# Conformer block on one core: eight input loads are moved behind other DMA reads on one queue

## The chip, the cores and the metric

The kernel runs on one core of a Trainium2 chip. Its engines work side by side, each through its own list of instructions: TensorE (PE, matrix products; PEld is its loading of weights), VectorE (DVE), ScalarE (ACT), GpSimd (POOL), and SyncE (SP), which here does nothing but issue DMA transfers. They wait for each other through semaphores. The metric is device microseconds of the whole program.

## The reference

One conformer block over x of shape (2, 4000, 144): two batches of 4000 tokens of 144 features, 4 heads of 36.

```
x = x + 0.5 * (silu(layernorm(x) @ w_ff1a) @ w_ff1b)
q, k, v = split(layernorm(x) @ w_qkv)               # 4 heads of 36
x = x + softmax(q k^T * 36**-0.5) v @ w_o           # 4000 x 4000 scores per head
a, b = split(layernorm(x) @ w_pw1)
c = depthwise_conv(a * sigmoid(b), dw)              # 5 taps along the tokens
x = x + silu(c) @ w_pw2
x = x + 0.5 * (silu(layernorm(x) @ w_ff2a) @ w_ff2b)
return layernorm(x)
```

## The kernel before

**Tiles.** Tokens are cut into 16 chunks of 500, chunks 0 to 7 for the first batch and 8 to 15 for the second; a chunk is four blocks of 125 tokens on 125 partitions. All of x lies on the chip in one tile X. Each chunk goes through layer norm, the first feed-forward and the q, k, v products ("pre"), then attention, then convolution and the second feed-forward. Attention is by far the largest part: TensorE makes scores (PS<-QT,KT), ScalarE, and for a part of the tiles VectorE, makes exponentials out of them (PT<-PS), and TensorE multiplies those with the values (PS<-PT,VA). While the attention of the first chunks runs, the pre of later chunks is worked in between, and while the first batch's attention runs, the second batch's pre.

**Transposes.** TensorE needs the normalized chunk (XN, or AN for the attention's output) with features on partitions. After the first chunks this is done through DRAM by `blocks` (line 967): VectorE transposes 32 x 32 squares in place (STREAM_TRANSPOSE XN<-XN); SP then issues four DMA writes into a DRAM buffer `rows` (the order in which it stands there does the rest of the transposing), waits for them to land, and issues the DMA reads that bring the chunk back, two for each chunk. For the feed-forward and the convolution the reads go to a tile XT, one of five; for the q, k, v products to XTQ, one place for each of the eight chunks of a batch. All of these, the X loads and the output go out on SP's one queue, in SP's order.

**X loads.** Chunks 0 to 7 are loaded at the very start. Those of the second batch stand in the list `later` (line 837), in the order 9, 10, 8, 11, 12, 14, 15, 13. `blocks` counts its calls in `n_dma`. From the fourth call on, each call issues one load of the list, behind its four writes and ahead of its two reads:

```
for a in range(4): ...            # four writes  rows <- XN
n_dma[0] += 1
if n_dma[0] > 3 and later:
    load_x("sp", later.pop(0), cost=0.0, lat=0.0)
yield need("sp")
for dst, f0, f1, n, cost, lat in reads: ...   # two reads  XT or XTQ <- rows
```

The reads wait for the writes' semaphore; an X load waits for nothing but its turn on SP.

**Order.** Work is described by generators (threads) that a planner interleaves by modelled costs when the program is built. The order on each engine is then permuted by a table, ORDER (`R.reorder`, line 2039), so that on the chip each engine has a fixed list; nothing is decided at run time. An X load belongs to the same step as the writes or reads that it is emitted with, and is permuted with them. The recorder emits every instruction from one line, so the profile shows L377 for nearly all; tiles and operations tell them apart.

Of the kernel before, what the change touches and what calls it, by code (L numbers as in the profile page):

```python
# [133 lines left out]
def c_dve(n, rate=1.0):  # L134
    return n / (960 * rate) + 0.07
# [398 lines left out]
def bass_standalone__conformer_family_zipformer__speech_kernel(  # L534
# [258 lines left out]
    def load_x(eng, c, r=(), cost=0.45, lat=2.9):  # L793
        op(eng, "dma_start", X[0:TB, c * NB:(c + 1) * NB, :], x_tok[c], q=f"x{c}", r=r, w=[("X", c, i) for i in range(NB)],
           cost=cost, lat=lat)

    def load_ff(eng, qa, qb, WA, WE, WB, wa, wb, nm, la=None, lb=None):
        load_k(eng, qa, WA, wa[:, 0:512], (nm, "a", 0), (nm, "z", 0), la)
        load_k(eng, qa, WE[:, :, 64:128], wa[:, 512:FF], (nm, "a", 1), (nm, "z", 1), la)
        load(eng, qb, WB[:, 0:4, :], wb[0:512, :].rearrange("(t p) d -> p t d", p=128), [(nm, "b", 0)], lat=lb)  # L800
        load(eng, qb, WB[0:64, 4, :], wb[512:FF, :], [(nm, "b", 1)], lat=lb)
        load(eng, qb, WB[64:128, 5, :], wb[512:FF, :], [(nm, "b", 2)], lat=lb)
# [31 lines left out]
        load("sp", "w2", WP2Z[i * LC:(i + 1) * LC, i, :], w_pw2[ML:D, :], [("WP2Z", i)])  # L834
    load("sp", "w2", DWR[0:KCONV, 0:D], dw, ["DWR"])
    load_ff("sp", "w2", "w2", WA2, WE2, WB2, w_ff2a, w_ff2b, "W2")
    later = [9, 10, 8, 11, 12, 14, 15, 13]
    n_dma = [0]
    R.free["sp"] += 0.45 * len(later)

# [126 lines left out]
    def blocks(v, key, z, reads, q, wk):  # L967
        yield need("dve")
        op("dve", "transpose", v, v, r=[key], w=[key], cost=c_dve(320))
        yield need("sp")  # L970
        first, v = None, v.rearrange("p (g k n) -> p g k n", g=2, n=32)
        for a in range(4):
            args = "sp", "dma_start", DR[z, :, :, a, :, :].rearrange("k r g n -> r g k n"), v[32 * a:32 * a + 32, :, :, :]
            if first is None:
                first = op(*args, q=f"d{z}", r=[key], w=[("DR", z)], cost=W_COST, lat=W_LAT)
            else:
                R.more(first, [key], [("DR", z)], *args, q=f"d{z}", cost=W_COST, lat=W_LAT)
        n_dma[0] += 1
        if n_dma[0] > 3 and later:
            load_x("sp", later.pop(0), cost=0.0, lat=0.0)  # L980
        first, d = None, DR[z, :, :, :, :, :].rearrange("k r a g n -> (k r) g a n")
        yield need("sp")
        for dst, f0, f1, n, cost, lat in reads:
            args = "sp", "dma_start", dst, d[f0:f1, :, :, :].rearrange("f g a n -> f g (a n)")[:, :, 0:n]
            if first is None:
                first = op(*args, q=q, r=[("DR", z)], w=wk, cost=cost, lat=lat)
            else:
                R.more(first, [("DR", z)], wk, *args, q=q, cost=cost, lat=lat)

    def transp_q(u, c, bs, inter):  # L990
        cc, n = c % CPB, len(bs)
        wk = [("XTQ", cc, i) for i in bs]
        q_inter[c] = inter
        if inter:
            yield from blocks(
                XNF[:, u, :], ("XN", u), NXT + cc,
                [(XTQF[0:HD, k, cc, :, :], HD * k, HD * k + HD, TB, 0.855, 2.2) for k in range(2)], f"tq{cc}", wk)
            return
        bk = yield need("pe", banks, dur=0.11 * n)
        ps = PSH[0:HD, bk, 0:256 * n].rearrange("p (k i n) -> p k i n", k=2, i=n)  # L1000
        for k in range(2):
            for i in range(n):
                op("pe", "transpose", ps[:, k, i, 0:TB], XN[0:TB, u, i, k * HD:(k + 1) * HD], IDENT[0:TB, 0:TB],
                   r=[("XN", u), "ID"], w=[("ps", bk)], cost=0.055, kind="f")
        yield need("dve", hold=True)
        c0 = cc * CH + bs[0] * TB
        copy(XTQ[0:HD, :, c0:c0 + n * TB].rearrange("p k (i n) -> p k i n", i=n), ps[:, :, :, 0:TB], [("ps", bk)], wk,
             2 * n * TB, 2.0, flex())
        banks.give(bk)

    def transp(u, an, s, bs, inter, dma, rows=TB):
        n, key = len(bs), ("AN" if an else "XN", u)
        wk = [("XT", s, i) for i in bs]
        x_inter[s] = dma
        if dma and s not in xt_set:
            xt_set.add(s)
            op("pool", "memset", XT[0:LP, s, 1, :, :], 0.0, w=wk, cost=0.5)
        if dma:
            yield from blocks((ANF if an else XNF)[:, u, :], key, s,
                              [(XTF[0:128, s, 0, :, :], 0, 128, 128, 0.43, T_LAT), (XTF[0:16, s, 1, :, :], 128, D, 128, 0.43, T_LAT)], f"t{s}", wk)  # L1020
            return
        bk = yield need("pe", banks, dur=0.11 * n)
        ps = PSH[:, bk, 0:256 * n].rearrange("p (k i n) -> p k i n", k=2, i=n)
        kr = (128, 32 if inter else LP)
        for k in range(2):
            for i in range(n):
                b = bs[i] if an else i
                if inter:
                    src = (ANI if an else XNI)[0:rows, u, b // 2, 128 * k:128 * k + kr[k], b % 2]
                else:  # L1030
                    src = (ANS if an else XNS)[0:rows, u, b * D + 128 * k:b * D + 128 * k + kr[k]]
                op("pe", "transpose", ps[0:kr[k], k, i, 0:rows], src, IDENT[0:rows, 0:rows], r=[key, "ID"],
                   w=[("ps", bk)], cost=0.055, kind="s" if inter and k else "f")
        eng = flex()
        for k in range(2):
            yield need(eng, hold=True)
            copy(XT[0:kr[k], s, k, bs[0]:bs[-1] + 1, 0:rows], ps[0:kr[k], k, :, 0:rows], [("ps", bk)], wk, n * rows, 2.0,
                 eng)
        banks.give(bk)
# [1031 lines left out]
```

## Time and profile before

| | us |
|---|---|
| runs of the kernel before | 888.76, 888.76, 889.62 (median 888.76) |
| profiled execution, its own time | 894.72 |
| its span, first to last instruction | 892.8 |

| engine | busy us | share of the span | instructions |
|---|---|---|---|
| PE | 862.4 | 97% | 11478 |
| ACT | 852.4 | 95% | 1095 |
| DVE | 818.5 | 92% | 1799 |
| POOL | 303.2 | 34% | 584 |

Mean granted TensorE clock: 0.990.

How to read it: "busy" of PE counts a product from its start to its modelled end, at whatever clock was granted. A timeline row has its start, its length, the engine, the operation as out<-in, how many were merged, and in brackets the idle time just before it and what ended that. In the chain of waits "SPq" is SP issuing, "DMA" is a transfer on its way. A row of the table by stretches has the stretch, its length, then the busy time of PE, PEld, DVE, ACT and POOL with their instructions, and at the end the granted TensorE clock (1.00 is full), the mean busy share of the 16 DMA engines, and GB/s.

### The profile page before, as it was taken

To read this page: it belongs to the slowest core of one execution; us is meant where nothing else is said; L and a number is where in the kernel's file an instruction comes from. 1 tells how busy PE (TensorE), PEld (TensorE's weight loads), DVE (VectorE), ACT (ScalarE), POOL (GpSimd) and SP (SyncE) were. 2 spreads that over 40 slices of the span, in tenths; PEclk is the share of its full clock that TensorE was granted. 3 is DMA by queue.
4 is the path that set the end of the run, shared out by engine and by line. 5 is a ranking of instruction groups with operands and counts; after the bars stand their busy time and mean duration, and the time that the engine had idled before them with its cause. 6 is when DMAs were issued, how large, how long until landed. Compare 5 with 4: busy or idle time off the path is not lost.

```text
span 892.8 us, 27130 instructions
## 1 busy us (share of the span) xinstructions
PE 862.4 (97%) x11478; PEld 385.8 (43%) x11478; DVE 818.5 (92%) x1799; ACT 852.4 (95%) x1095; POOL 303.2 (34%) x584
## 2 busy tenths in 40 slices
PE   8989999999999999999999999999999999999996
PEld 7533333344344444344344444443434343444466
DVE  7956999999999999999988899998888999999987
ACT  6778999999999999999999999999999999999974
POOL 7761510214433333114106224241541017021733
PEclk9988999999999999999999999999999999999999
DMA  3230110111210210201101111002111001101101
GB/s 101 47 79 21 43 36 18 22 22 31 51 30 22 44 30 18 55 16 38 36 16 25 34 29 31 22 16 43 30 37 23 8 10 42 36 9 36 36 17 34
DMA packets 114222, 28.81 MB, mean 32 GB/s; under 512 B 101085, under 2 KB 114100, under 8 KB 114100
## 3 DMA queue, kind: packets, MB, share of 16 engines
q1 hardware_dynamic: 112642, 26.46, 13.5%
q8 instruction: 90, 1.47, 0.7%
q10 hardware_dynamic: 1458, 0.62, 0.3%
q14 instruction: 32, 0.26, 0.1%
HBM read 13.44 MB, written 13.61 MB: 30 GB/s over the span
## 4 chain that ended last, share of the span: by engine, by line
ACT 44%; PE 38%; DVE 15%; POOL 1%; DMA 1%; issue 1%; SPq 1%; DVEq 0%
ACT PT L377 39%; PE PS L377 38%; DVE PT L377 8%; ACT TH L377 4%; DVE ST L377 1%; DVE X L377 1%; DVE QT L377 1%; DVE XN L377 1%; DVE HT L377 1%; POOL XN L377 1%; DVE KT L377 1%; POOL RS L377 1%; SPq L377 1%; DMA X<-in_x_dram 0%; DVE AN L377 0%
## 5 line engine op out<-in xcount | busy, mean ns | idle before, releaser
L377 ACT ACTIVATE PT<-PS 128x1000 bf16<-128x1000 f32 (+1 forms) x822 | 756.6, 1066 | 10.8 <-PE PS L377 9.6
L377 PE MATMUL PS<-QT,KT 64*64 64x500 bf16 x3968 | 427.4, 387 | 14.0 <-ACT PT L377 8.3
L377 PE MATMUL PS<-PT,VA 64*37 64x500 bf16 x4712 | 412.1, 374 | 2.0 <-DVE PT L377 0.7
L377 DVE TENSOR_SCALAR PT<-PS 128x500 int16<-128x500 f32 x372 | 244.3, 668 | 8.0 <-PE PS L377 6.5
L377 PEld LDWEIGHTS PS<-QT,KT 64*64 64x64 bf16 x3968 | 124.7, 104 | 241.5 <-ACT PT L377 135.0
L377 POOL TENSOR_SCALAR RS<-ST 125x4 f32<-125x4 f32 x130 | 35.2, 271 | 467.3 <-DVE ST L377 461.1
L377 PEld LDWEIGHTS PS<-PT,VA 64*37 64x37 bf16 x4712 | 141.1, 96 | 97.0 <-DVE PT L377 21.4
L377 POOL TENSOR_SCALAR XN<-X,RS 125x144 bf16<-125x144 bf16 x260 | 152.7, 621 | 7.4 <-DMA out_dram<-XN 0.7
L377 DVE TENSOR_SCALAR PT<-PT 128x1000 uint16<-128x1000 uint16 x372 | 150.6, 416 | 1.9 <-PE PS L377 0.5
L377 DVE TENSOR_TENSOR PT<-PT 128x1000 bf16<-128x1000 bf16 x186 | 126.3, 681 | 1.4
L377 ACT ACTIVATE TH<-PS 128x500 bf16<-128x500 f32 (+3 forms) x198 | 105.0, 553 | 4.5 <-PE PS L377 3.2
L377 POOL TENSOR_TENSOR RS<-RS,NHALF 125x4 f32<-125x4 f32 (+1 forms) x93 | 91.5, 987 | 37.4 <-DVE RS L377 31.5
L377 DVE SCALAR_TENSOR_TENSOR HT<-TH,PS 128x500 bf16<-128x500 bf16 (+1 forms) x135 | 80.7, 616 | 17.3 <-ACT TH L377 16.4
L377 PE MATMUL PS<-XT,WA 128*128 128x500 bf16 (+4 forms) x288 | 75.3, 366 | 0.4
L377 DVE BATCH_NORM_STATS2 ST<-X 125x6 f32<-125x288 bf16 x160 | 65.5, 445 | 2.9 <-DMA X<-in_x_dram 2.7
L377 DVE SCALAR_TENSOR_TENSOR X<-PS,X 125x288 bf16<-125x288 f32 (+1 forms) x128 | 57.1, 451 | 10.0 <-PE PS L377 8.9
L377 PE MATMUL PS<-WB,HT 128*125 128x144 bf16 (+1 forms) x640 | 51.9, 230 | 0.6 <-ACT HT L377 0.4
L377 PEld LDWEIGHTS PS<-WB,HT 128*125 128x125 bf16 (+1 forms) x640 | 44.2, 136 | 14.0 <-issue 4.8
L377 PEld LDWEIGHTS PS<-XT,WA 128*128 128x128 bf16 (+1 forms) x288 | 21.2, 98 | 34.4 <-issue 12.8
L377 POOL COPY U<-U 128x2 bf16<-128x2 bf16 (+1 forms) x54 | 11.6, 254 | 71.4 <-DVE U L377 71.4
L377 PE MATMUL PS<-U,DG 128*128 128x375 bf16 (+6 forms) x204 | 29.0, 264 | 0.2 <-DVE PT L377 0.2
L377 DVE STREAM_TRANSPOSE XN<-XN 128x320 f32<-128x320 f32 x54 | 27.0, 499 | 1.7 <-POOL XN L377 1.6
(93 smaller groups left out, 535.4 us busy)
## 6 DMA issues: line engine op xcount, KB each, us to landing
rows<-XN SPq DMA_DIRECT2D x216, 40.0 KB, 2.0
XT<-rows SPq DMA_DIRECT2D x56, 128.0 KB, 2.0
rows<-AN SPq DMA_DIRECT2D x60, 40.0 KB, 2.0
X<-in_x_dram SPq DMA_DIRECT2D x16, 140.6 KB
XTQ<-rows SPq DMA_DIRECT2D x26, 70.3 KB
out_dram<-XN SPq DMA_DIRECT2D x13, 140.6 KB
XT<-rows SPq DMA_DIRECT2D x56, 16.0 KB, 1.9
out_dram<-XN SPq DMA_DIRECT2D x3, 70.3 KB
```

The costliest lines, as they stand in the source:

```text
L377: ins = getattr(eng, o.name)(*o.a, **o.k)
```

## The change

The load no longer stands between a transpose's writes and its reads. It stands behind the reads, and each load of the list now carries the number of the call of `blocks` from which it may go: 9, 10 and 8 at the eighth call, 11 at the eleventh, 12 and 14 at the thirteenth, 15 at the fifteenth, 13 at the sixteenth.

```diff
-    later = [9, 10, 8, 11, 12, 14, 15, 13]
+    later = [(9, 8), (10, 8), (8, 8), (11, 11), (12, 13), (14, 13), (15, 15), (13, 16)]
...
     # blocks(), behind the four writes
-        n_dma[0] += 1
-        if n_dma[0] > 3 and later:
-            load_x("sp", later.pop(0), cost=0.0, lat=0.0)
     # the two reads
...
+        n_dma[0] += 1
+        while later and later[0][1] <= n_dma[0]:
+            load_x("sp", later.pop(0)[0], cost=0.0, lat=0.0)
```

In the order on SP, where the trace of before has a load behind the writes that start at 41.59, 48.96, 52.10, 59.63, 62.81, 90.25, 100.60 and 122.47 us, there is none now. Chunks 9, 10 and 8 follow one another behind the XTQ reads of 67.13, 11 stands behind the XT reads of 126.43, 12 and 14 behind those of 159.87, 15 behind the XTQ reads of 179.53 and 13 behind the XT reads of 199.20. The lists of PE, DVE, ACT and POOL hold the same operations in the same order; at a few places two of the XN buffers are exchanged.

## The prediction

> **What bounds the kernel now.** I read the page first, then busy time by stretches, then the chain of waits and the timelines of the queues around the one odd place. The page:
>
> ```profile
> span 892.8 us, 27130 instructions
> ...
> PEclk9988999999999999999999999999999999999999
> ...
> ACT 44%; PE 38%; DVE 15%; POOL 1%; DMA 1%; issue 1%; SPq 1%; DVEq 0%
> ```
>
> ScalarE and TensorE share the chain that ended last; DMA is 1% of it. TensorE's granted clock dips once inside the program (third and fourth slice of 22.3 us) before the end. Cut into stretches (columns: time of PE, PEld, DVE, ACT, POOL, then granted clock):
>
> ```profile
> 58.10:60.34 2.24, 0.00 (x1) 0.01 (x1) 0.46 (x1) 1.21 (x2) 2.24 (x3) 0.91 0.41 125
> 59.94:73.60 13.66, 13.26 (x130) 4.43 (x130) 4.84 (x9) 7.43 (x9) 1.50 (x2) 0.50 0.33 75
> 73.60:76.33 2.73, 2.73 (x30) 0.80 (x26) 1.18 (x3) 2.57 (x5) 0.00 (x0) 1.00 0.00 0
> 76.33:850.00 773.67, 757.06 (x10264) 318.44 (x10252) 728.37 (x1529) 769.51 (x945) 241.66 (x455) 1.00 0.13 29
> ```
>
> TensorE does nothing for 2.24 us, then runs 13.66 us at a clock of 0.50, busy throughout. From 76.33 to 850 ScalarE is busy 769.51 of 773.67 us: there the kernel is bound by ScalarE's work in its fixed order, and what that stretch begins with, it ends with. So a microsecond won before 76.33 is a microsecond at the end. What ScalarE lost before that:
>
> ```profile
> L377 ACT ACTIVATE PT<-PS 128x1000 bf16<-128x1000 f32 x8 | 7.8, 1003 | 6.2 <-PE PS L377 6.2
> L377 ACT ACTIVATE TH<-PS 128x500 bf16<-128x500 f32 x3 | 1.7, 588 | 0.5 <-PE PS L377 0.5
> L377 ACT ACTIVATE KT<-PS 128x500 bf16<-128x500 f32 x1 | 0.6, 587 | 0.3 <-PE PS L377 0.3
> ```
>
> These are ScalarE's groups between 61.9 and 76.3: 10.1 us of work with 7.0 us of idle time, all ended by TensorE.
>
> The first wait has its cause in the SP queue. The chain of waits there, then TensorE's own rows:
>
> ```profile
> 54.04 1.60 SPq L377
> ...
> 57.17 3.12 DMA XTQ<-rows
> ```
> ```profile
> 57.71 0.38 PE L377 MATMUL PS<-QT,KT 64*64 64x500 bf16 x4
> 60.34 1.02 PE L377 MATMUL PS<-XTQ,WK 72*128 72x500 bf16 x2 [2.24 <-DMA XTQ<-rows]
> ```
> ```profile
> 74.67 0.63 PE L377 MATMUL PS<-XT,WA 128*128 128x500 bf16 x2
> ```
>
> TensorE was ready at 58.10 (57.71 + 0.38) and waited for the XTQ read that landed at 60.29.
>
> **The change, part by part.** Eight X loads move on SP; no other engine's order changes. SP, in order of time:
>
> ```profile
> 48.96 2.55 SPq L377 DMA_DIRECT2D rows<-XN  x4
> 51.55 0.51 SPq L377 DMA_DIRECT2D X<-in_x_dram  x1
> 52.10 3.54 SPq L377 DMA_DIRECT2D rows<-XN  x4
> 55.69 0.51 SPq L377 DMA_DIRECT2D X<-in_x_dram  x1
> 56.23 3.35 SPq L377 DMA_DIRECT2D XTQ<-rows  x4
> ...
> 67.13 1.69 SPq L377 DMA_DIRECT2D XTQ<-rows  x2
> 90.25 2.60 SPq L377 DMA_DIRECT2D rows<-XN  x4
> ...
> 199.20 0.82 SPq L377 DMA_DIRECT2D XT<-rows  x2
> 206.91 2.55 SPq L377 DMA_DIRECT2D rows<-XN  x4
> ```
> ```profile
> 50.49 0.50 DVE L377 STREAM_TRANSPOSE XN<-XN 128x320 f32<-128x320 f32 x1
> ```
>
> *What it removes.* The X loads at 51.55 (chunk 10) and 55.69 (chunk 8) stand between the writes and the reads of the two transposes that TensorE waits for. Without the first, the second write may start at 51.55: its data was ready at 50.99. That is 0.55. Those four issues took 3.54 where an undisturbed write takes 2.55 (the row at 48.96); the chain shows the 1.60 of the last one. I put that on the load just ahead of it, so 0.99 goes. Without the second load another 0.54. The read is then issued at 56.23 - 0.55 - 0.99 - 0.54 = 54.15.
>
> How long it takes is bounded from both sides. Four such issues take 3.35, so the second of the pair goes out 0.84 later, at 54.99. The nearest rows for its landing are the same read in this trace, behind a load (3.12 after its issue, 57.17 to 60.29), and the undisturbed reads of the other transposes, the XT reads at 29 to 31 us:
>
> ```profile
> DMA to landing us min/median/max: 1.9/1.9/1.9
> ```
>
> So it lands between 56.9 and 58.1. I take 57.5, the middle: it is a read of other shape than XT's, but the load that delayed it is gone. TensorE needs it at 58.10, so at either end the 2.24 us go whole or to within 0.1.
>
> *The half clock.* It begins at 59.94, 1.84 us into TensorE's only long wait. I take the wait as its cause: without it, TensorE runs through this stretch at 1.00. The rule that speaks against this is in the Trainium skill, "TensorE: Matmul & The Clock Gate", section "Why this matters for your kernels": no gaps over about 3 us, since "One MID window of idle" drops the clock. Its Part 1 also has the full clock back after one busy window of about 3.4 us. By the rule a gap of 2.24 us would not do it, and a drop would cost some 1.7 us, an estimate from that page; at most 2.24 + 1.7 = 3.9 us would be won. The trace differs on both: 1.84 us idle came just before the drop, and 13.66 us followed. The measurement decides here.
>
> *The two together.* On TensorE, what was 58.10 to 76.33 (18.23 us) becomes half of 13.26 plus 2.73, that is 9.36, if nothing else limits it: 8.9 us less. ScalarE sets the nearer limit:
>
> ```profile
> 57.34 1.97 ACT L377 ACTIVATE PT<-PS 128x1000 bf16<-128x1000 f32 x2
> ...
> 85.48 44.93 ACT L377 ACTIVATE PT<-PS 128x1000 bf16<-128x1000 f32 x49
> ```
>
> It was done with its last exponential at 59.31 and reached 76.33 in 17.02 us. Undisturbed its eight PT take 44.93 / 49 = 0.917 each, 7.3 us; with 2.3 for TH and KT that is 9.6. So 17.02 - 9.6 = 7.4 us are won. The bound from above is TensorE's 8.9; from below, if only the wait goes and the clock stays, 2.24.
>
> *What is late next.* The read of the next transpose (XT, used by TensorE at 74.67) stands behind the SP write whose data comes from these two VectorE steps, which themselves waited for TensorE:
>
> ```profile
> 61.39 0.68 DVE L377 CAST KT<-PS 128x500 bf16<-128x500 f32 x1 [2.84 <-PE PS L377]
> 61.99 0.50 DVE L377 STREAM_TRANSPOSE XN<-XN 128x320 f32<-128x320 f32 x1
> ```
>
> In the changed kernel: cast at 58.10 + half of 1.05 = 58.6, transposed 0.60 + 0.50 later at 59.7, written by 62.3, second read issued 0.4 later (two took 0.82 at 199.20) and landed 1.9 after that, 64.6. TensorE comes there at 58.10 + 6.63 + 1.07 (74.67 less 73.60) = 65.8. Margin 1.2 us: I count nothing for it, but it is thin.
>
> *What it adds.* Three X issues (1.6 us on SP) right behind the XTQ read at 67.13. The next write behind them waits until 90.25, so SP stands idle for 21.4 us there, and both ends move alike. The other five go behind reads at later places; the tightest is the one behind 199.20, with 6.9 us until the next write. A load is quick against that, and needed late:
>
> ```profile
> 0.74 3.75 DMA X<-in_x_dram
> ```
> ```profile
> 97.46 0.81 DVE L377 BATCH_NORM_STATS2 ST<-X 125x6 f32<-125x288 bf16 x2
> ```
> ```profile
> 222.25 0.77 DVE L377 BATCH_NORM_STATS2 ST<-X 125x6 f32<-125x288 bf16 x2
> ```
>
> 97.46 is the first use of any of the three (chunk 8). Even with no lead they land by 68.82 + 1.6 + 3.75 = 74.2, 23 us before it, and both move alike. 222.25 is the first use of the fourth (chunk 11) and of any later one; the last of the eight is issued behind the read at 199.20. All this costs nothing; if the cover were gone, VectorE would wait in its fixed order and all behind it. The loads that stood after 76.33 stood where ScalarE hardly starves, by the stretch above, and the remaining ones before it delay reads that TensorE doesn't wait for here, so I count no gain for them.
>
> *Sum.* -2.24 and the half clock, together -7.4 at ScalarE; nothing added. Against the profiled execution's own 894.72 (span 892.8 and 1.9 around it) that is 887.3. The runs shown have a median of 888.76, 6.0 under the profiled one; I carry the difference over: 888.76 - 7.4 = 881.4.
>
> **The rivals.**
>
> *The clock is not won.* (a) The gap is not the cause of the half clock: 1.84 us are too short for it, something else halves the clock all the same, and ScalarE stays starved by it. Only the wait goes: 888.76 - 2.24 = 886.5. Against: one drop inside the program and one wait of this length in these rows, side by side. (This is what the skill's rule above would make of it.) (b) The runs shown never had the half clock: 6.0 us under the profiled run is close to what it costs. Then again only the wait goes, 886.5. For: that closeness. Against: the gap comes from the queue's order, which every run shares, and the three times lie within 0.9 us.
>
> *The read comes late anyhow.* If the 1.60 us issue and the 3.12 us read come from the transposes' own traffic, only the two load issues go (1.09): the read lands at 60.29 - 1.09 = 59.2, a wait of 1.1 us stays, and if the clock falls over it too, about 1 us is won: 887.7, hardly to be told from no change (a measurement of this kernel can tell about 0.2%, 1.8 us).
>
> *Slower.* The half clock moves to the XT read of 64.6 against 65.8. Should it land 3.0 us later than worked out, TensorE waits 1.8 us, as long as what came before the drop in this trace. If the runs shown had no half clock before, they get one: half of 13.26, less the wait that went: 888.76 + 6.6 - 2.24 = 893.1. For: the margin is 1.2 us and the chain runs through three engines. Against: no load is left near it, and its steps are short.
>
> **How the numbers follow.** The forecast, 881.4, has a chance of 0.62; (a) 0.08 and (b) 0.14, both at 886.5; the late read 0.08; slower 0.08. The likeliest case alone spans 878.1 (TensorE's 8.9 us, and for each of the two medians the 0.86 by which the runs shown differ) to 882.6 (the 1.2 us of the thin margin gone). The range reaches on to 886.5 and half that 0.86: 878.1 to 887.0, leaving out 0.16. Faster by over 0.2% is 0.62 + 0.22 = 0.84, within 0.2% 0.08, slower 0.08.
>
> **What would show it.** Right: SP's XTQ read issued near 54.2, no wait of TensorE over 0.5 us between 57 and 66, a granted clock of 1.00 from 50 to 80, ScalarE's idle time there near zero, and its long run of exponentials (85.48 here) some 7 us earlier. Wrong: a clock of 0.50 anywhere before the end, TensorE waiting on XT near 65, VectorE waiting on an X load, or the lead shrinking between 76 and 850.

## The result, and the profile after

The changed kernel takes 887.5 us (median of 14 runs, 887.03 to 888.41). The kernel before, run beside it 14 times, took 888.53 to 895.17, median 890.75; the ratio is 0.9958, with a 95% interval of 0.9942 to 0.9975. So it is faster, by much less than forecast, and 887.5 lies above the range. The two profiled executions differ by what was forecast: 894.72 before, 887.44 after, 7.28 us against 7.4. By their times, the three runs of before that the forecast started from (median 888.76) and this profiled execution belong to two different groups of runs, as the clocks of later runs show; most of what follows is about that.

Of the page of the changed kernel:

```profile
span 885.6 us, 27130 instructions
...
PEclk9999999999999999999999999999999999999999
...
ACT 43%; PE 39%; DVE 14%; POOL 1%; DMA 1%; SPq 1%; issue 1%; DVEq 0%; POOLq 0%
```

The dip of TensorE's clock in the third and fourth slice is gone. By stretches (the columns of before), before's 0.50 is now 1.00 and ScalarE is busy 13.46 us where it was 7.43:

```profile
59.94:73.60 13.66, 13.42 (x193) 5.18 (x192) 8.53 (x16) 13.46 (x17) 1.76 (x2) 1.00 0.32 76
```

ScalarE's groups between 61.9 and 76.3; the 7.0 us of idle time are 0.2:

```profile
L377 ACT ACTIVATE PT<-PS 128x1000 bf16<-128x1000 f32 x14 | 13.2, 1044 | 0.2 <-PE PS L377 0.2
L377 ACT ACTIVATE TH<-PS 128x500 bf16<-128x500 f32 x4 | 2.4, 646 | 0.0
L377 ACT ACTIVATE KT<-PS 128x500 bf16<-128x500 f32 x1 | 0.6, 593 | 0.0
```

SP's timeline after, then two pieces of its chain of waits, then TensorE's rows that waited for a DMA:

```profile
49.22 5.20 SPq L377 DMA_DIRECT2D rows<-XN  x8
54.46 4.15 SPq L377 DMA_DIRECT2D XTQ<-rows  x4
```
```profile
54.46 1.68 SPq L377
...
56.18 2.56 DMA XTQ<-rows
```
```profile
58.79 0.59 PE L377 MATMUL PS<-XTQ,WK 72*128 72x500 bf16 x2 [0.44 <-DMA XTQ<-rows]
69.96 0.59 PE L377 MATMUL PS<-XTQ,WK 72*128 72x500 bf16 x2 [0.24 <-DMA XTQ<-rows]
```

The eight writes stand without a load between them, the read goes out at 54.46, but its first issue takes 1.68 us, and 0.44 of the 2.24 us of waiting is left. ScalarE's long run of 69 exponentials, before and then after, starts 7.14 us earlier and is as long:

```profile
85.48 62.45 ACT L377 ACTIVATE PT<-PS 128x1000 bf16<-128x1000 f32 x69
```
```profile
78.34 62.43 ACT L377 ACTIVATE PT<-PS 128x1000 bf16<-128x1000 f32 x69
```

### The profile page after: what moved, and what is told of

Same layout as the page of the kernel before. It is cut to its first block, busy times and chain, and to the rows that moved or that the text cites. A ratio compares the mean times of both kernels' runs of the same rounds, so it can differ in the third digit from the quotient of the medians.

```text
span 885.6 us, 27130 instructions
## 1 busy us (share of the span) xinstructions
PE 857.2 (97%) x11478; PEld 385.1 (43%) x11478; DVE 818.4 (92%) x1799; ACT 851.5 (96%) x1095; POOL 303.9 (34%) x584
## 4 chain that ended last, share of the span: by engine, by line
ACT 43%; PE 39%; DVE 14%; POOL 1%; DMA 1%; SPq 1%; issue 1%; DVEq 0%; POOLq 0%
ACT PT L377 39%; PE PS L377 39%; DVE PT L377 8%; ACT TH L377 4%; DVE ST L377 1%; DVE HT L377 1%; DVE X L377 1%; POOL XN L377 1%; DVE QT L377 1%; DVE XN L377 1%; DVE KT L377 1%; SPq L377 1%; DMA XTQ<-rows 1%; POOL RS L377 0%; DVE VA L377 0%
```

## Experiments

My first theory: a wait of TensorE that is long enough halves its clock, whatever work is in it, and before has such a wait in some of its executions only. Its rivals: the half clock comes from something else in that stretch, or every execution of before has it. The expectations stand as they were given, ahead of each group of runs.

**Before again.** No edit.

> The kernel before, unchanged, run again. Theory A (a lottery over the clock): TensorE's wait of about 2.2 us at the XTQ read is there in every execution, but the half clock follows only in some, by where the wait falls in the clock's window. Then the runs form two groups, near 889 us with a mean granted clock of about 0.998 and near 893 to 895 us with about 0.990, and nothing between 890.5 and 891.5 that lacks a lower clock. Theory B (the spread is not the clock): the times between 888.5 and 895 do not follow the granted clock. If the profiled execution is one without half clock, theory A expects it to show the wait of about 2.2 us and a time near 889 us.

Measured: 889.9 median of 12 (888.44 to 894.46), ratio 0.9995 (0.9973 to 1.0018). It is two groups: seven runs at 888.44 to 889.97 with a mean granted clock of 0.998 or 0.999, five at 892.68 to 894.46 with 0.991 or 0.992. Over all 105 runs of before that stood beside the experiments, 59 had a clock of 0.996 or more and took 887.63 to 889.98, 41 took 892.5 to 895.0, and 5 lay between at 0.993 or 0.994. The profiled execution had the half clock. By stretches:

```profile
57.35:60.76 3.41, 1.19 (x18) 0.23 (x6) 1.00 (x2) 1.88 (x3) 3.41 (x5) 1.00 0.38 115
60.76:71.01 10.25, 10.25 (x112) 3.76 (x112) 4.05 (x7) 5.95 (x7) 0.60 (x2) 0.50 0.41 94
```

The first row is the 3.41 us just before the drop (TensorE busy 1.19, idle 2.22), the second the drop, 10.25 us long: three times 3.41. In the trace of before it was 13.66, four times.

**The wait filled, and made longer.** e3: before, with 32 products that nobody reads put into TensorE's list ahead of the product that waits. e9: 26 more ahead of the next wait, for XT. e8: before, with loads 11 and 12 also ahead of the first XTQ read.

```diff
+    fill_wait(R, "tq3", 32, IDENT)   # e3, e9: unread products ahead of the one that waits for XTQ
+    fill_wait(R, "t1", 26, IDENT)    # e9 alone: the same ahead of the one that waits for XT
```
```diff
-    # load behind the writes of each call from the fourth on: 9, 10, 8, 11, 12, 14, 15, 13
+    mid = {4: [9], 5: [10], 6: [8, 11, 12], 9: [14], 10: [15], 11: [13]}     # e8
```

> The kernel before with 32 products of 128 x 128 that nobody reads put ahead of the one that waits for the XTQ read, so TensorE is busy for about 1.8 of the 2.2 us. The read, and with it the loss to ScalarE, stays. Theory A: a granted clock of about 0.998 in every run, all runs between 888.3 and 890 us, none above 891; slower than the changed kernel's 887.5 by 1 to 2 us. Theory B: runs up to 895 us as before.

> The kernel before with unread products put ahead of both waits, 32 ahead of the first XTQ read and 26 ahead of the XT read behind it. Theory A: no window with over 1.3 us of idle time, so no half clock in any run: clock 0.997 or more throughout, one group at 888.3 to 889.8 us, where the kernel filled at the first wait alone had 888.6 to 891.6 and the kernel before 888.3 to 894.8. The late reads themselves stay, so it does not reach the changed kernel's 887.5.

> The kernel before with the loads of 11 and 12 moved to stand behind that of 8, ahead of the first XTQ read: two more issues and transfers there, none behind the next transposes. Theory A: the wait grows from 2.2 to 4 us or more, longer than one clock window of 3.41 us, so that some window has over 1.5 us of idle time wherever it begins: a granted clock of 0.990 to 0.993 in every run, no run near 889, all at 893 to 897 us. If the clock were no matter of the wait's length, the same two groups as before, each later by 2 us.

e3: 889.48 (888.6 to 891.62), ratio 0.9984 (0.9966 to 1.0003). No run above 891.62, but five at 890.9 or more, which I had not expected. Its profiled execution shows why: the filled wait was gone, and TensorE waited at the next late read, which halved the clock for one step of 3.41 us:

```profile
70.53 1.85 PE L377 MATMUL PS<-XT,WA 128*128 128x500 bf16 x4 [1.74 <-DMA XT<-rows]
```
```profile
66.88:70.29 3.41, 1.91 (x23) 0.61 (x22) 1.54 (x3) 2.76 (x4) 0.00 (x0) 1.00 0.39 116
70.29:73.71 3.42, 3.19 (x20) 1.08 (x24) 1.35 (x2) 1.89 (x3) 0.00 (x0) 0.50 0.05 14
```

e9, with both waits filled: 890.15 (889.46 to 891.26), ratio 0.9991 (0.9972 to 1.0011), one group with clocks of 0.997 to 0.999 in all 12 runs. Of the 105 runs of before, 46 had 0.994 or less. The loads stood where they were, and SP went on to issue the two reads late: in the profiled execution the first XTQ read at 55.68 and the first XT read at 66.96 (54.46 and 63.94 in the changed kernel, 56.23 and 66.17 in before). Only TensorE had no gap, with at most 0.04 us idle in any step of 3.41 between 53 and 74 us. That takes the loads' place in the queue and the DMA traffic out as direct causes of the half clock. It lies 1.8 us above the runs of before beside it that had no half clock (median 888.39), more than expected: the fillers take time of their own. e8: 895.38 (893.91 to 895.78), ratio 1.0045 (1.0026 to 1.0063), the half clock in all ten runs (0.990 to 0.992). The wait had been expected at 4 us or more and was 3.05:

```profile
61.60 0.60 PE L377 MATMUL PS<-XTQ,WK 72*128 72x500 bf16 x2 [3.05 <-DMA XTQ<-rows]
```

With a longer wait the half clock came in every run, with no gap in none: the wait is the cause.

**Parts of the change.** e1: only 9, 10 and 8 moved. e2: only the five others moved. e5 and e6: the changed kernel with one load put back behind its writes.

```diff
+    mid = {7: [11], 8: [12], 9: [14], 10: [15], 11: [13]}   # e1; later = [(9, 8), (10, 8), (8, 8)]
+    mid = {4: [9], 5: [10], 6: [8]}                         # e2; later without these
+    mid = {5: [10]}                                         # e5; later without 10
+    mid = {6: [8]}                                          # e6; later without 8
```

> Only the loads of chunks 9, 10 and 8 go behind the XTQ reads of the eighth call; 11, 12, 14, 15 and 13 stay between writes and reads as before. Theory A1 (the loads of 10 and 8 ahead of the first XTQ read are all of it): 887.5 us, clock 0.998, as the changed kernel. Theory A2 (TensorE, no longer held at the first XTQ read, meets the next late reads, XT and XTQ behind the loads of 11 and 12): a wait of 1.5 to 2.5 us there, at about 66 us, some runs at half clock, 888.5 to 894 us. Theory C (the later loads bring the gain): 889 to 894 us with the wait at the first XTQ read as before.

> The other half: 9, 10 and 8 stay between writes and reads as before, 11, 12, 14, 15 and 13 go behind reads as in the changed kernel. Theories A1 and A2: the wait of about 2.2 us at the first XTQ read stays, and with it the two groups, near 889 and near 893 to 895 us. Theory C: 887.5 us in every run.

> The changed kernel with one load, chunk 10, put back between the writes of the two transposes (where it stood at 51.55). The prediction's term for it is 0.55 for the issue and 0.99 for the slowed write, 1.5 us at the read: then TensorE waits 0.44 + 1.5 = 1.9 us at the first XTQ read, ScalarE is 1.5 us later, fast runs near 889.0 us, and some runs fall to half clock (893). Rival: the slowed write is made up by what SP and the read wait for anyway; then only 0.5 us at most, a wait under 1.0 us, 887.5 to 888.0 us, and no half clock.

> The changed kernel with one load, chunk 8, put back right ahead of the first XTQ read (where it stood at 55.69). The prediction's term: 0.54 for the issue and up to 1.2 for the read behind it. If the two terms add up, this one and that of chunk 10 together make the 1.7 us (2.14 less 0.44) by which the wait is longer with both, so here 0.44 + 0.2 to 0.7. If they do not add up, this load alone makes a wait of 1.5 us or more, 888.5 to 889 us, with half clock in some runs.

e1: 890.58 (888.43 to 893.6), ratio 0.999 (0.9971 to 1.0009). With the first wait gone, TensorE waits for XT behind loads 11 and 12, and six of 12 runs lie at 891.0 or more, with clocks of 0.992 to 0.997:

```profile
68.52 1.09 PE L377 MATMUL PS<-XT,WA 128*128 128x500 bf16 x4 [1.62 <-DMA XT<-rows]
```

So the loads between 59 and 66 us, for which I counted no gain, are needed: moving the front three alone gives no gain that these runs can tell. At the first XTQ read e1 did what the prediction said: SP's first issue took 0.89, the second read went out at 55.22 and landed at 57.60, and TensorE did not wait for it. e2: 888.22, ratio 0.9982 (0.9959 to 1.0005), eight runs at 887.62 to 888.85, four at 892.65 to 893.55. Its profiled execution had the whole wait and no half clock, because the wait fell across the border of two steps of 3.41 us, with 1.31 idle in the one and 0.83 in the other:

```profile
60.45 0.59 PE L377 MATMUL PS<-XTQ,WK 72*128 72x500 bf16 x2 [2.14 <-DMA XTQ<-rows]
```
```profile
56.20:59.62 3.42, 2.11 (x26) 0.77 (x24) 1.70 (x4) 3.32 (x5) 3.24 (x7) 1.00 0.37 92
59.62:63.03 3.41, 2.58 (x25) 0.71 (x27) 1.66 (x3) 1.60 (x2) 2.01 (x2) 1.00 0.38 83
```

(The borders are counted back in steps of 3.413 us from the clock's drop at the end. The step is worked out from the traces' clock records, whose stretches between two changes are whole multiples of it: 10.24 us is three, 13.65 four, 54.61 sixteen.) e5: 887.91, ratio 0.9974 (0.9955 to 0.9993), one run of 12 with the half clock, a wait of 0.79; e6: 887.38, ratio 0.9972 (0.9956 to 0.9989), a wait of 0.50 at this place, which the profile puts down to VectorE, and no run with the half clock. One load put back costs 0.4 us or nothing, where I had expected more of load 10. With both (e2) the wait was 2.14 us, but e2's profiled execution, like e5's, also has a slow write (1.56 and 1.39 us instead of 0.6), which the next runs show to come by chance.

**Why only some executions.** Before twice more, for a profiled execution without the half clock; e10 is one.

> The kernel before, unchanged, one profiled execution, to see one without the half clock. If the half clock falls on about half of all executions, this one has either no dip inside the program, about 888.5 us, a wait of 2.1 to 2.3 us at the first XTQ read, and ScalarE's run of 69 exponentials about 1.2 to 1.7 us later than in the changed kernel (79.5 to 80.0); or a dip after the wait and 892.5 to 894.5 us. If the wait always brings the half clock down and the faster executions have a shorter wait, an execution without the dip shows a wait under 1.5 us.

> The same kernel as the one beside it, a second execution: the same two outcomes, with the same numbers. Without the dip, the wait of 2.1 to 2.3 us lies across a border of the clock's steps of 3.41 us, with under 1.5 us of it in either step; with the dip, 1.5 us or more of idle time lies in the step just before it.

e10: 889.73 us at 0.998. Its rows on SP, in the chain of waits and on TensorE, and ScalarE's long run:

```profile
52.58 2.55 SPq L377 DMA_DIRECT2D rows<-XN  x4
```
```profile
59.64 0.59 PE L377 MATMUL PS<-XTQ,WK 72*128 72x500 bf16 x2 [1.06 <-DMA XTQ<-rows]
69.26 1.08 PE L377 MATMUL PS<-XT,WA 128*128 128x500 bf16 x4 [0.94 <-DMA XT<-rows]
```
```profile
80.04 62.49 ACT L377 ACTIVATE PT<-PS 128x1000 bf16<-128x1000 f32 x69
```

The wait is 1.06, not the 2.1 to 2.3 expected, and the four writes took 2.55 although the same load stands ahead of them: there is no slow issue. e11 (894.01 us at 0.993) had the slow issue, four writes in 3.76, a wait of 2.06 with 1.97 us idle in one step, and the half clock.

So the slow SP issue comes and goes. In the DMA queues' view, cut to 0.2 us where the slow write goes out in before (54.00 to 54.20), and to 54.80 to 55.00 in e10:

```profile
q8 instruction: 1, 0.02, 36.7%
...
rows<-XN SPq DMA_DIRECT2D x1, 40.0 KB, 3.0
```
```profile
q8 instruction: 1, 0.02, 40.8%
```

Queue q8 brings instructions, 16 KB at a time, 90 times in before; TensorE has 22,956 products and weight loads, about 255 for each. Over the first twelve traces, 170 of the 3,312 writes from `rows<-XN` and `rows<-AN` took over 0.8 us instead of 0.6, and such a load was under way beside every one of the 170. Where it started from 0.5 us before the issue to 0.1 behind it, 138 of 178 were slow; where more than 1.0 before or 0.3 behind, none. In before's three profiled executions with the half clock, and in e2, it starts at 54.00 to 54.40, with the fourth write; in e10 at 54.89, late in that write and ahead of the X load, whose issue took its usual 0.50. To test this, the number of TensorE's instructions ahead of that place was changed, by warm-up products that nobody reads, at about the same busy time:

```diff
-    # 50 warm-up products 128x128 at the start, 29 more at 12 us
+    refill(R, PSV, IDENT, (0, 0), 8)    # e12: before, 8 more, narrower: 16 instructions more
+    refill(R, PSV, IDENT, (11, 3), 0)   # e13: before; e14: changed. 56 made into 14 wide ones: 84 fewer
```

> Kernel before with 8 more of the unread warm-up products at the start, each narrower so that they take as long together: 16 more TensorE instructions. If a load of TensorE's instructions (one for each 256) is what makes an SP issue slow when both start together, the load that falls at 54.0 to 54.9 now falls some 0.55 us earlier (16 of 256 instructions that take 8.8 us), at 53.4 to 54.4, among the writes in every execution: a slow write, a wait of TensorE of 2.1 to 2.3 us, and the half clock in nearly every run: at least 9 of 12 runs at a clock under 0.995 and 892.5 to 895, median above 892. If the lottery has another cause, about half of the runs stay at 888.0 to 890, median 888.3 to 891.

> Kernel before with 42 fewer warm-up products: 56 of them made into 14 of four times the width, 84 TensorE instructions fewer in about the same time. The load of instructions then falls some 2.9 us later, at 57.0 to 57.8, behind the issue of the read that TensorE waits for. If it is the cause: no write over 0.7 us between 49 and 56, a wait of 1.0 to 1.1 us, no half clock in any run, all at 0.996 or above, 887.8 to 889.9, median 888.5. If the lottery has another cause: both groups as before, 4 or more of 12 runs at 892 to 895.

> Changed kernel with the same 84 instructions fewer. If the load of instructions is what makes its first XTQ read slow to issue (1.68 us) and late (58.75): that issue takes 0.8 to 0.9, the second read lands at 57.5 to 57.9 as forecast, no wait of TensorE over 0.1 us there, and the median is 0.3 to 0.5 us under that of the changed kernel beside it, 886.9 to 887.3. If the slow issue comes from eight writes in a row: 1.2 to 1.7 us for that issue as before, a wait of 0.3 to 0.5, and the same time as the changed kernel to within 0.2.

> The changed kernel, unchanged, beside the other three: 887.0 to 888.4, clocks of 0.997 or above, median 887.5.

e12: median 893.32; nine of 12 runs at 891.75 to 894.03 with clocks of 0.992 or 0.993, as many as expected, though two of them lie under the 892.5, against 14 of 35 runs of before beside it (13 above 892.5, one at 0.994). The ratio, 1.0006 (0.9985 to 1.0026), doesn't tell; the share of runs with the half clock is higher, but 12 runs show that only weakly. Its profiled execution was one of the other three, with the load at 53.67 and a slow write all the same (1.17), and it shows where the border lies: 1.49 us idle in one step, and no drop.

```profile
59.45 0.60 PE L377 MATMUL PS<-XTQ,WK 72*128 72x500 bf16 x2 [1.49 <-DMA XTQ<-rows]
```
```profile
56.21:59.62 3.41, 1.92 (x25) 0.66 (x24) 1.34 (x3) 2.96 (x4) 3.23 (x7) 1.00 0.39 106
```

e13: the first wait came out as expected, 1.03 with the four writes in 2.55. But the load now fell at 59.02 instead of 57.0 to 57.8, and the one after it at 66.05, with the XT reads:

```profile
52.02 2.55 SPq L377 DMA_DIRECT2D rows<-XN  x4
...
65.70 1.66 SPq L377 DMA_DIRECT2D XT<-rows  x2
```
```profile
58.86 0.59 PE L377 MATMUL PS<-XTQ,WK 72*128 72x500 bf16 x2 [1.03 <-DMA XTQ<-rows]
...
69.03 1.08 PE L377 MATMUL PS<-XT,WA 128*128 128x500 bf16 x4 [1.01 <-DMA XT<-rows]
```

The time missed its expectation: median 892.42, ratio 1.0023 (1.0004 to 1.0042), nine of 12 runs at a clock of 0.996 or less. The profiled one had none, so that the XT wait brings it in the others is likely, not shown.

e14 beside e15: the first XTQ issue took 0.90 instead of 1.68 (e15: 1.62), and the read landed 2.50 behind the second issue. But one of the eight writes ahead of it was now slow, so it came at 58.39 and not at 57.5 to 57.9; and a write of the next chunk was slow too (1.37). The second XT read went out 0.48 later than in the changed kernel's first trace and took 3.28 instead of 2.63 to land, so TensorE waited for XT:

```profile
58.44 0.60 PE L377 MATMUL PS<-XTQ,WK 72*128 72x500 bf16 x2 [0.23 <-DMA XTQ<-rows]
68.39 1.09 PE L377 MATMUL PS<-XT,WA 128*128 128x500 bf16 x4 [1.28 <-DMA XT<-rows]
```

e14 took 888.88 (ratio to before 0.9984, 0.9968 to 1.0), e15 887.12 (0.9963, 0.9947 to 0.9979). The profiled executions of the two are 1.0 us apart (spans of 886.6 and 885.6), and 0.8 of that is there when ScalarE's long run begins (79.18 against 78.39), behind the XT wait. Eight writes in a row are not what makes the issue slow; the load of instructions goes on to hit the next thing that SP issues. No version measured clearly below the changed kernel.

## Why the prediction was wrong, by its steps

**Right.** The wait as the cause of the half clock (e8, e9). The sum for the profiled execution, 7.4 against 7.28, by the same ScalarE bound: after the change ScalarE ended the exponential that ended at 59.31 before at 59.57, 0.26 later, and began its long run 7.14 earlier, 7.40 in all. A microsecond before 76 us is one at the end: the lead of 7.14 us at the long run of exponentials is 7.2 in the spans (892.8 and 885.6). The XTQ issue at 54.15: measured 54.46. No later load cost anything: the lead at ScalarE stayed between 7.1 and 7.2 us to the end, and the only wait that the profile puts down to an X load is VectorE's first one, at the very start (2.7 us before, 2.9 after).

**The step that failed: "I carry the difference over".** The 7.4 us contained a half clock that the three runs with the median of 888.76 did not have, by their times: their clocks are not on record, but of the 105 later runs of before every one under 890 us had a clock of 0.996 or more. It was bad luck in part: with 59 of 105 runs in that group, three in a row come from it about one time in six. Rival (b) said so, its evidence (6.0 us under the profiled execution) was in the text, and I gave it 0.14 because "the gap comes from the queue's order, which every run shares". That reason was wrong: the order is shared, but how long one issue takes is not. Against the group without the half clock, the change wins 1.4 us (888.92, the median of the seven runs under 890 beside it, less 887.5) and 1.9 beside e15 (888.99 less 887.12); against the other group 5.0 to 7.5 (892.5 to 895.0). The measured 0.9958 is a mixture of the two.

**Rival (b) itself was mis-sized too**, at 886.5. It took off the wait of 2.24 us, but without the half clock before's wait is 1.06 here and 0.94 at XT (e10). The long run of exponentials starts 1.70 us earlier after the change than in e10, and 5.44 earlier in e10 than in the profiled execution of before: the first is the gain over this execution without the half clock, the second what the chance was worth between these two (half clock and longer wait together).

**"I put that on the load just ahead of it, so 0.99 goes."** It did not go away. The slow issue belongs to a load of TensorE's instructions that starts beside it: in e10 the four writes take 2.55 with the same X load ahead. In the changed kernel it moved from the fourth write to the XTQ read: the second read went out at 56.18 instead of 54.99, of which 0.31 is the later start and 0.88 the slow issue, and it landed 2.56 us after that, where I had taken 2.51. So 57.5 became 58.74, and 0.44 us of waiting are left, since TensorE was ready at 58.35. In e1, without the slow issue, the read landed at 57.60.

**The rule that spoke against it.** The Trainium skill, "TensorE: Matmul & The Clock Gate", section "Why this matters for your kernels", warns only of gaps over about 3 us, and its Part 1 has the full clock back after one busy window. Here 1.50 us idle within one step of 3.41 dropped the clock in e3, and 1.49 did not in e12; the drop lasted one, three or four steps. The measurements decide, as I had taken it; what I lacked is that a gap so near the border falls on either side of it from one execution to the next. Nor is 1.5 us of idle time a rule for all work, as the end of the changed kernel's own trace shows (last section).

**"What is late next" and the slower rival.** The late XT read is real (1.74 in e3, 1.62 in e1, 1.28 in e14), but in the changed kernel's trace TensorE just did not wait there: the second XT read landed at 67.21 and TensorE came at 67.40, so the margin was 0.2 us, not 1.2. The landing at 64.6 was 2.6 too early, because it has the write start at 59.7, when its data is ready: SP was then still issuing four other writes (from 58.66), so this one went out from 61.30 to 63.90, and the second read behind it had a slow issue and landed 2.63 us after its start. That TensorE came 1.6 later too is what saved it. In e1 the loads 11 and 12, for which I counted nothing, stand ahead of this read and make it late, and the change moves them as well; in e14 a slow write and a slower landing did it without them.

**Left open.** Why the drop lasts one, three or four steps; and why a load of instructions that starts within an issue slows it in about three of four cases and not in all.

## What to carry to other kernels

Before a gain is worked out on a profiled execution, see whether that execution belongs to the same group as the times: a mean clock of 0.990 beside a median 6 us lower says that it does not, and then the gain is to be worked out for each group and weighed. A gap of TensorE near 1.5 us is worth closing even where it is short, because the half clock that it may bring cost more than the gap itself here, and only by chance: the medians of the two groups of before are 888.63 and 893.23, 4.6 us apart, for a wait of about 1 us in the profiled execution of the faster group (e10) and about 2 in those of the slower one. A DMA issue that is slow in one trace is not thereby caused by its neighbour in the queue; look at what else moves at that moment, the loads of instructions among it.

## What the runs showed of the hardware

In these traces TensorE's clock changes in steps of 3.413 us: every drop inside the program lasted one, three or four of them, and began a whole number of them behind the first entry of the trace's clock record (5.33 us in before, and 59.94 is sixteen steps later). The idle time in the step just before was 1.50 (e3), 1.85 (before), 1.97 (e11), 2.22 (e4) and 2.88 (e8) where it dropped, and at most 1.49 (e12), 1.31 (e2) and 1.10 (e1) in any step between 54 and 74 us where it did not. There TensorE works mostly on products with 64 rows. At the end of the program, with products of 128 rows, 1.83 us idle did not bring the drop in the changed kernel, where the next step is still at 1.00; 2.09 (e8) and 2.11 (e12) did. So the border near 1.5 us holds for the work in this stretch, and what counts besides idle time is open:

```profile
876.98:880.39 3.41, 1.58 (x26) 1.43 (x24) 3.31 (x14) 0.69 (x2) 1.92 (x3) 1.00 0.14 42
880.39:883.81 3.42, 0.00 (x0) 0.00 (x0) 0.74 (x4) 0.00 (x0) 0.15 (x1) 1.00 0.27 77
```

A drop of four steps, with the longer wait that brought it, was worth 5.4 us at ScalarE here.

A 16 KB load of TensorE's instructions, once for about 255 of them, made the SP issue beside which it started slow in about three of four cases: a write took 0.8 to 2.1 us instead of 0.6, and the first XTQ read of the changed kernel 1.62 and 1.68 instead of 0.9. The number of TensorE instructions ahead thus moves a stall on another engine's queue: 84 fewer, with the same transfers in the same order, made the changed kernel 1.8 us slower (888.88 against 887.12).
